# A linear-attention and GELU feed-forward kernel on one core: the first product of each pair slot reads its weights from another place in the ring

## The chip, the cores and the metric

The kernel runs on one core of a Trainium2 chip. The metric is device time in microseconds (us); lower is better. A profile is one execution recorded by the hardware; its times are us unless marked ns. TensorE does the matmuls (PE in the profile; its weight loads, which run beside matmuls, are PEld), VectorE is DVE, ScalarE is ACT, GpSimd is POOL, and SyncE is SP, whose queue issues the transfers here.

## What is computed

Per head, `kv = k^T v`, `out = q kv`, an RMS norm over the 64 head columns with a gain, and then a feed-forward layer with GELU over all 4608 tokens:

```python
kv = np.einsum('bhsd,bhse->bhde', k, v)          # batch 8, heads 8, seq 576, head_dim 64
out = np.einsum('bhsd,bhde->bhse', q, kv)
rms = np.sqrt(np.mean(out * out, axis=-1, keepdims=True) + 1e-06)
x = (out / rms * g_norm) as (4608, 512)
h = x @ w_in                                      # 512 x 2048
g = 0.5 * h * (1.0 + erf(h / sqrt(2)))
return g @ w_out                                  # 2048 x 512
```

## The kernel before

**Tiles and stages.** The 4608 tokens are nine chunks of 512 (CH). A weight block of `w_in` is 128 of the 2048 hidden columns, 16 blocks in all; `w_out` has 16 blocks likewise, which stay on the chip. For accuracy every operand is kept as two float32r parts, a high one and the rest (hi, lo), and a product takes three matmuls: hi by hi, lo by hi, hi by lo.

**The two plain chunks (c = 0, 1).** The first layer (line 537) multiplies whole blocks; the second layer (line 563) adds into four PSUM tiles `acc`. In chunk 1, TensorE and VectorE also form sums and differences of quarters of `w_in`, and SP stores them as 28 tiles `products` in device memory (lines 366 to 419).

**The pair chunks (c = 2 to 8).** From chunk 2 on, two blocks of the first layer are taken together as a pair, with seven products of half size in place of eight (Strassen's scheme in Winograd's form). There are 8 pair slots a chunk and 7 chunks, 56 slots. In a slot, `layer1_pair` (line 429) runs products 0 to 6 in order. Product k takes six matmuls of line 444: two halves of the contraction, three part products each. The stationary operand (`lhsT`, 128x128) is a quarter block of the weights from `products`; the moving operand (`rhs`, 128x256) is a piece of x. After the slot's seven products come the second layer's matmuls of earlier blocks (line 563, 128x512, mostly 24), in some slots a projection of the next chunk (line 218) or sums for kv (line 158). VectorE combines the products in PSUM meanwhile (lines 436 and 454), and ScalarE applies GELU (lines 549, 550).

**Which tiles are moving operands.** `piece_tile` (line 359) gives them: in even chunks product 0 reads x2, product 1 x3 and the others w_in5 to w_in9, in odd chunks product 0 to 3 read x0, x1, x4, x5 and the others w_in10 to w_in12. The names w_in4 and up are old weight tiles used again.

**The ring.** The weights of the products come back through a ring of RING = 4 tiles, w_in0 to w_in3. Each is 1024 + ROOM = 1088 elements of 4 bytes a partition. One transfer of 512 KB fills a tile with two products in a row, numbers n = 2t and 2t + 1 of the whole run, at the elements AWAY = 48 to 48 + 1024. So product n stands 192 bytes into its tile if n is even, and 192 + 2048 if it is odd. `load_products(t)` (line 423) is called for tile t + 4 when the second product of tile t has been written out as code, so the transfer waits on TensorE for that product's end. As a slot has seven products, product 0 of a slot is the first half of a tile in every second slot and the second half in the others.

**Addresses.** In the built program the four ring tiles and all the tiles with moving operands start at byte addresses that leave the same remainder, 192, on division by 256; so do the `w_out` tiles and the GELU results gh and gl, the operands of lines 563 and 584. Blocks inside tiles start at multiples of 512 bytes from there.

**What sets the order.** The schedule is written by hand. Each engine runs its instructions in program order and waits on semaphores. SP issues all transfers in program order: the ring loads, the kv and q loads of later chunks (lines 103 to 193) and the output stores (line 605). The transfers take the semaphores DMAHW0 to DMAHW7 in turn, so a transfer may have to wait until an earlier one with its semaphore has landed.

**The end.** `finish` (line 569) runs the last chunk's last blocks; its last output tile is done in two halves of 256 columns, 12 matmuls of 128x256 on line 584, with gh or gl as stationary and `w_out` as moving operand.

Of the kernel before, what the change touches and what calls it, by code (L numbers as in the profile page):

```python
# [8 lines left out]
F32 = mybir.dt.float32  # L9
# [15 lines left out]
RING = 4  # L25
# [11 lines left out]
def linear_attn_rms_gelu_ffn(  # L37
# [16 lines left out]
    nc = tc.nc  # L54
    ctx.enter_context(tc.manual_schedule())
    NT, DM = out.shape
# [26 lines left out]
    AWAY, ROOM = 48, 64  # L83
# [265 lines left out]
    NPR = len(OPERANDS)  # L349
    NT2 = NPR * NF // 4  # L350
    kept = {}

    def reused(i, dtype=F32):

        if i not in kept:
            kept[i] = block_tile(f"w_in{i}", dtype)
        return kept[i][:, :2 * DM]
# [6 lines left out]
    products = [dram.tile([P, 2 * DM], F32, name=f"products{t}") for t in range(NT2)]  # L364
# [56 lines left out]
    ring = {}  # L421

    def load_products(t):
        if t < (NCH - PLAIN) * NT2:
            reused(t % RING, F32R)
            ring[t] = kept[t % RING][:, AWAY:AWAY + 2 * DM]
            nc.sync.dma_start(out=ring[t].bitcast(F32), in_=products[t % NT2])

    def layer1_pair(at, j, between):


        a, b = (ps_h.tile([P, CH], F32, name="ps_h") for _ in range(2))
        left, right = slice(0, HALF), slice(HALF, CH)
        u = reused(15).rearrange("p (a n) -> p a n", n=HALF)
        p1, u2, v, u3 = (u[:, i] for i in range(4))
        add = lambda out, x, y: nc.vector.tensor_tensor(out=out, in0=x, in1=y, op=ALU.add)  # L436

        def product(k, out, first=False):
            n = ((at.c - PLAIN) * NF // 2 + j) * NPR + k
            w, x = ring[n // 2][:, n % 2 * DM:(n % 2 + 1) * DM], at.x[k]  # L440
            for kb in range(2):
                hi, lo = (w[:, m * HALF + kb * P:m * HALF + (kb + 1) * P] for m in range(2))
                for i, (y, z) in enumerate(((hi, 0), (lo, 0), (hi, 1))):
                    nc.tensor.matmul(  # L444
                        out=out, lhsT=y, rhs=x[:, z, kb], start=first and kb + i == 0,
                        stop=kb == 1 and i == 2, skip_group_check=True,
                    )
            if n % 2:
                load_products(n // 2 + RING)

        between[0]()
        product(0, a[:, left], True)
        product(1, a[:, right])
        nc.vector.tensor_copy(out=p1, in_=a[:, left])  # L454
        add(v, a[:, right], p1)
        product(2, b[:, right], True)
        product(3, b[:, left])
        add(u2, b[:, right], p1)
        between[1]()
        product(4, a[:, left])  # L460
        product(5, a[:, right])
        add(a[:, right], a[:, right], u2)
        product(6, b[:, right])
        add(u3, b[:, right], p1)
        add(b[:, left], b[:, left], u3)
        add(b[:, right], b[:, right], v)
        return a, b
# [141 lines left out]
    first, second = attn[:2]  # L609
# [49 lines left out]
    for d in range(0, 2 * D, BLK):  # L659
        h = d // D * D  # L660
        nc.gpsimd.tensor_tensor(
            out=fold[:, d:d + BLK], in0=ident[:, h:h + BLK], in1=ident[:, h + BLK:h + 2 * BLK],
# [25 lines left out]
    n = 2 * NB  # L688


    def sum_squares(p):
# [13 lines left out]
        out=half_g, in0=ps[:, :1], scalar1=0.5, scalar2=None, op0=ALU.mult  # L705
# [3 lines left out]
        out=sums[:, :P], lhsT=ones, rhs=eps, start=True, stop=False,  # L709
# [4 lines left out]
        out=root_g, in0=half_g, scalar1=D ** 0.5, scalar2=None, op0=ALU.mult  # L714
# [8 lines left out]
    for p in (2, 3):  # L723
# [5 lines left out]
        out=sums[:, :n].rearrange("p (g b) -> p g b", g=2), lhsT=fold, rhs=first.part[:, :2, :],  # L729
# [3 lines left out]
    for p in (2, 3):  # L733
        nc.scalar.activation(
            out=first.o_tile(p), in_=first.ps.pop(p), func=AF.Copy, scale=root_g
# [9 lines left out]
    for p in (2, 3):  # L745
        bcs[p] = ps_acc.tile([P, DM], F32, name=f"acc{p}")
        for t in range(NG):
            for h, r in enumerate((slice(0, D), slice(D, 2 * D))):
                k = n + 2 * ((p - 2) * NG + t) + h
                nc.tensor.matmul(  # L750
                    out=bcs[p][r, t * P:(t + 1) * P],
# [3 lines left out]
    for p in range(2):  # L755
# [3 lines left out]
            out=first.o_tile(p), in0=first.ps.pop(p), scalar=root_g, in1=bc, op0=ALU.mult,  # L759
# [86 lines left out]
    def later(c, i):  # L846

        if i == 9:
            sums[c] = attn[c + 1].fold()
        if i in (5, 7):  # L850
            load_kv(c + 2, (i - 5) // 2)
        if i == 9:
            attn[c + 2].load(0)
        if i == 13:
            for p in (2, 3):
                load_kv(c + 2, p)
        if i == 15:
            attn[c + 2].load(1)
        if i == 13:
            for t in range(RING):  # L860
                load_products(t)
# [36 lines left out]
    for s in range(PLAIN * NF):  # L898
# [36 lines left out]
        else:  # L935
# [3 lines left out]
            n = 0 if not 1 <= i <= 11 else 2 if i in (1, 3, 5, 7, 11) else 1  # L939
# [114 lines left out]
```

## Time and profile before

| What | Value |
| --- | --- |
| Median of 3 runs | 830.99 us (830.6 to 831.09) |
| The profiled execution | 830.12 us |
| Its span, first to last instruction | 828.3 us |
| Granted TensorE clock | 1.000 over the span |
| Ring loads (line 427) | 196 of 512 KB, median 4.6 us from issue to landing |
| Products written (line 370) | 40 and 16 of 256 KB |

How to read it. A row of a group gives line, engine, operation, what is written `<-` what is read (with buffer numbers left out), the shape and the count; then durations. Matmuls overlap their neighbours, since they are pipelined, so the duration of one says less than the distance from one start to the next. The chain of waits follows the work that ended last back through what released it; its rows in order of time are start, length and how many instructions. A row of a timeline is start, length and instructions merged. In a row of transfers, "landing" counts from the issue on the queue to the semaphore that tells of the last byte.

### The profile page before, as it was taken

The numbers are of one execution on the slowest core, as the hardware profiler recorded it, in microseconds if no ns is written. First come the engines' busy times: TensorE is split into PE (matmuls) and PEld (weight loads), VectorE is DVE, ScalarE is ACT, GpSimd is POOL, SyncE is SP. The second block draws the span as 40 slices with busy tenths as digits, with TensorE's granted clock in tenths as the row PEclk, the third lists the DMA queues.
The fourth block names the chain that finished last, engine by engine and source line by source line (L and its number), as shares of the span: only waits on it lengthen the run. The fifth ranks groups of instructions, "written<-read, shape, count | busy, mean of one in ns | idle before, by whom it ended". The sixth has DMA issues, their size and how long they took to land.

```text
span 828.3 us, 13810 instructions
## 1 busy us (share of the span) xinstructions
PE 823.5 (99%) x5390; PEld 730.1 (88%) x5390; DVE 496.3 (60%) x980; ACT 314.0 (38%) x578; POOL 65.7 (8%) x69
## 2 busy tenths in 40 slices
PE   9999999999999999999999999999999999999998
PEld 7688888888999999999999999999999989999997
DVE  3999838687546744675457544673467456744443
ACT  3788444434531334233423253233323332322221
POOL 1000021001010100010100110010101000100000
PEclk9999999999999999999999999999999999999999
DMA  9981337776684568555945688456445665556551
GB/s 352 406 334 51 115 127 248 253 262 241 228 318 129 184 237 306 177 178 204 327 163 176 204 276 279 140 176 238 171 173 177 227 202 178 178 178 229 178 178 51
DMA packets 61605, 174.97 MB, mean 211 GB/s; under 512 B 6500, under 2 KB 15460, under 8 KB 61540
## 3 DMA queue, kind: packets, MB, share of 16 engines
q1 hardware_dynamic: 61536, 174.09, 60.2%
q8 instruction: 43, 0.70, 0.3%
q14 instruction: 22, 0.18, 0.1%
q10 hardware_dynamic: 4, 0.00, 0.0%
HBM read 149.95 MB, written 24.12 MB: 210 GB/s over the span
## 4 chain that ended last, share of the span: by engine, by line
PE 99%; DVE 0%; issue 0%; ACT 0%; DVEq 0%
PE acc L563 48%; PE ps_h L444 33%; PE ps_h L537 10%; PE ps_a L218 3%; PE ps_a L158 2%; PE ps_h L529 1%; PE ps_h L648 1%; PE acc L682 0%; PE acc L750 0%; PE ps_h L694 0%; PE ps_a L248 0%; DVE w L602 0%; DVE sq L591 0%; DVE z L592 0%; ACT w L595 0%
## 5 line engine op out<-in xcount | busy, mean ns | idle before, releaser
L563 PE MATMUL acc<-w_out,gh 128*128 128x512 f32 x700 | 216.7, 391 | 0.0
L444 PE MATMUL ps_h<-w_in,w_in 128*128 128x256 f32 x1392 | 172.9, 279 | 0.0
L444 PEld LDWEIGHTS ps_h<-w_in,w_in 128*128 128x128 f32 x1392 | 167.8, 188 | 0.0
L563 PE MATMUL acc<-w_out,w_in 128*128 128x512 f32 x672 | 159.3, 391 | 0.0
L563 PEld LDWEIGHTS acc<-w_out,gh 128*128 128x128 f32 x700 | 129.2, 188 | 25.2
L563 PEld LDWEIGHTS acc<-w_out,w_in 128*128 128x128 f32 x672 | 123.9, 188 | 24.6
L563 PE MATMUL acc<-w_out,gl 128*128 128x512 f32 x350 | 136.4, 390 | 0.0
L549 ACT ACTIVATE gh<-ps_h 128x512 fp32r<-128x512 f32 x88 | 52.6, 597 | 209.2 <-DVE ps_h L436 153.4
L444 PEld LDWEIGHTS ps_h<-x,w_in 128*128 128x128 f32 x960 | 120.9, 188 | 4.3
L444 PE MATMUL ps_h<-x,w_in 128*128 128x256 f32 x960 | 122.2, 279 | 0.0
L454 DVE COPY w_in<-ps_h 128x256 f32<-128x256 f32 x56 | 23.8, 425 | 131.5 <-PE ps_h L444 131.5
L549 ACT ACTIVATE w_in<-ps_h 128x512 fp32r<-128x512 f32 x56 | 33.5, 598 | 182.0 <-DVE ps_h L436 182.0
L436 DVE TENSOR_TENSOR ps_h<-ps_h,w_in 128x256 f32<-128x256 f32 x168 | 72.7, 432 | 46.1 <-PE ps_h L444 42.2
L436 DVE TENSOR_TENSOR w_in<-ps_h,w_in 128x256 f32<-128x256 f32 x168 | 71.4, 425 | 46.8 <-PE ps_h L444 44.9
L537 PE MATMUL ps_h<-x,w_in 128*128 128x512 f32 x360 | 86.8, 390 | 0.0
L550 ACT ACTIVATE ps_h<-ps_h 128x512 f32<-128x512 f32 x144 | 85.5, 594 | 0.0
L555 DVE TENSOR_TENSOR gl<-ps_h,gh 128x512 fp32r<-128x512 f32 x88 | 60.4, 687 | 41.6 <-ACT ps_h L550 37.3
L537 PEld LDWEIGHTS ps_h<-x,w_in 128*128 128x128 f32 x360 | 67.4, 188 | 14.0 <-POOL x L306 0.2
L563 PEld LDWEIGHTS acc<-w_out,gl 128*128 128x128 f32 x350 | 65.7, 188 | 14.3 <-DVE gl L555 0.3
L555 DVE TENSOR_TENSOR w_in<-ps_h,w_in 128x512 fp32r<-128x512 f32 x56 | 38.4, 686 | 17.1 <-ACT ps_h L550 17.1
L206 POOL TENSOR_TENSOR ql<-q,qh 128x512 fp32r<-128x512 f32 x16 | 21.3, 1330 | 209.3 <-ACT qh L205 139.4
L341 POOL TENSOR_TENSOR w_in<-o,w_in 128x512 fp32r<-128x512 f32 x13 | 16.9, 1321 | 209.7 <-ACT w_in L336 209.7
(153 smaller groups left out, 641.3 us busy)
## 6 DMA issues: line engine op xcount, KB each, us to landing
w_in<-products SPq DMA_DIRECT2D x196, 512.0 KB, 4.6
products<-w_in SPq DMA_DIRECT2D x40, 256.0 KB, 3.3
w_in<-w_in SPq DMA_DIRECT2D x16, 512.0 KB, 10.2
kv_main<-kv_main SPq DMA_DIRECT2D x16, 512.0 KB, 6.9
w_out<-w_out SPq DMA_DIRECT2D x16, 512.0 KB, 10.2
q<-qT SPq DMA_DIRECT2D x15, 512.0 KB, 6.1
out<-w SPq DMA_DIRECT2D x18, 256.0 KB, 2.1
out<-z SPq DMA_DIRECT2D x17, 256.0 KB, 2.3
```

Of the source, the lines that this page charges most:

```text
L158: nc.tensor.matmul(out=ps[r, n * D:(n + 1) * D], lhsT=k[:, r], rhs=v[:, r], start=(j == 0), stop=(j == NJ),)
L206: eng.tensor_tensor(out=ql, in0=q, in1=qh.bitcast(F32), op=ALU.subtract)
L218: nc.tensor.matmul(out=ps[:, a:e], lhsT=w, rhs=x[:, a:e], start=(m == 0), stop=(m == 2))
L341: eng.tensor_tensor(out=x[:, 1], in0=self.block(OPERANDS[n]), in1=x[:, 0].bitcast(F32), op=ALU.subtract,)
L436: add = lambda out, x, y: nc.vector.tensor_tensor(out=out, in0=x, in1=y, op=ALU.add)
L444: nc.tensor.matmul(out=out, lhsT=y, rhs=x[:, z, kb], start=first and kb + i == 0, stop=kb == 1 and i == 2, skip_group_check=True,)
L454: nc.vector.tensor_copy(out=p1, in_=a[:, left])
L537: nc.tensor.matmul(out=h, lhsT=parts["in", i][:, w][:, p * P:(p + 1) * P], rhs=at.x[p][:, x], start=(m + p == 0), stop=(m == 2 and p == NP ...
L549: nc.scalar.activation(out=gh, in_=h, func=AF.Gelu)
L550: nc.scalar.activation(out=h, in_=h, func=AF.Gelu)
L555: nc.vector.tensor_tensor(out=gl, in0=h, in1=gh.bitcast(F32), op=ALU.subtract)
L563: nc.tensor.matmul(out=ps, lhsT=x[:, ts], rhs=parts["out", i][:, w], start=(i == 0 and m == 0), stop=(m == 2 and (i == NF - 1 or (i, t) == ...
```

## The change

`load_products` treats a tile that holds a slot's product 0 (n divisible by NPR = 7) in another way. Product 0 is put at the place that a tile without the shift of 48 elements would give it: at element 0 if it is the first half, and at 512 + ROOM = 576 if it is the second, byte 2304, which is nine times 256. Its neighbour in the tile stays where it was, 48 or 560 elements in. As the two halves are no longer one stretch, such a tile is loaded in two transfers of 256 KB. All other tiles are loaded as before. The ring now holds one view for each product, which `product` takes out by its number.

```diff
     def load_products(t):
         if t < (NCH - PLAIN) * NT2:
             reused(t % RING, F32R)
-            ring[t] = kept[t % RING][:, AWAY:AWAY + 2 * DM]
-            nc.sync.dma_start(out=ring[t].bitcast(F32), in_=products[t % NT2])
+            to, src = kept[t % RING], products[t % NT2]
+            first = [not n % NPR for n in (2 * t, 2 * t + 1)]
+            for a in range(2):
+                at = a * DM + (a * ROOM if first[a] else AWAY)
+                ring[2 * t + a] = to[:, at:at + DM]
+            if any(first):
+                for a in range(2):
+                    nc.sync.dma_start(
+                        out=ring[2 * t + a].bitcast(F32), in_=src[:, a * DM:(a + 1) * DM]
+                    )
+            else:
+                nc.sync.dma_start(out=to[:, AWAY:AWAY + 2 * DM].bitcast(F32), in_=src)
...
             n = ((at.c - PLAIN) * NF // 2 + j) * NPR + k
-            w, x = ring[n // 2][:, n % 2 * DM:(n % 2 + 1) * DM], at.x[k]
+            w, x = ring.pop(n), at.x[k]
```

In the changed file the lines behind this place stand ten further down, so line 444 becomes 454 and line 563 becomes 573.

TensorE's instructions keep their order. At the start of the second slot of chunk 2, where product 0 is the second half of a ring tile (w_in with a number; x_1971 is its moving operand), they were, with the semaphores each waits for in brackets:

```order
L563 MATMUL acc_1368<-w_out_1224,gl 128x512
L444 MATMUL ps_h<-x_1971,w_in_2051 128x256 [waits DVE_49,PE_49]
L444 MATMUL ps_h<-x_1971,w_in_2051 128x256 x5
L444 MATMUL ps_h<-x_2068,w_in_1483 128x256 [waits DMAHW1_49]
L444 MATMUL ps_h<-x_2068,w_in_1483 128x256 x5
L444 MATMUL ps_h<-w_in_2071,w_in_1483 128x256 [waits DVE_49]
```

and they are now:

```order
L573 MATMUL acc_1368<-w_out_1224,gh 128x512 x2
L573 MATMUL acc_1368<-w_out_1224,gl 128x512
L454 MATMUL ps_h<-x_1971,w_in_2052 128x256 [waits DMAHW1_49,DVE_49,PE_49]
L454 MATMUL ps_h<-x_1971,w_in_2052 128x256 x5
L454 MATMUL ps_h<-x_2070,w_in_1483 128x256 [waits DMAHW3_49]
L454 MATMUL ps_h<-x_2070,w_in_1483 128x256 x5
L454 MATMUL ps_h<-w_in_2073,w_in_1483 128x256 [waits DVE_49]
```

Product 0 has a wait of its own for the transfer of its half (DMAHW1); before, the product ahead of it in the same tile had waited for the whole.

On SP, at the first kv loads of chunk 2 (products with a number are the 28 tiles in device memory, 81 the first), there stood:

```order
L427 DMA w_in_2051<-products_88 128x1024 [waits DMAHW0_49,PE_49]
L427 DMA w_in_1483<-products_89 128x1024 [waits DMAHW1_49,PE_49]
L427 DMA w_in_1492<-products_90 128x1024 [waits DMAHW2_49,PE_49]
L427 DMA w_in_2049<-products_91 128x1024 [waits DMAHW3_49,PE_49]
L124 DMA kv_main<-kv_main 128x1024 [waits DMAHW4_49]
L141 DMA kv_tail<-kv_tail 128x256 [waits DMAHW5_49]
L124 DMA kv_main<-kv_main 128x1024 [waits DMAHW6_49]
L141 DMA kv_tail<-kv_tail 128x256 [waits DMAHW7_49]
L103 DMA z<-kv_main 128x512 [waits DMAHW0_49,DVE_49]
```

and now:

```order
L433 DMA w_in_2052<-products_88 128x512 [waits DMAHW2_49,PE_49]
L433 DMA w_in_2052<-products_88 128x512 [waits DMAHW3_49,PE_49]
L437 DMA w_in_1483<-products_89 128x1024 [waits DMAHW4_49,PE_49]
L437 DMA w_in_1492<-products_90 128x1024 [waits DMAHW5_49,PE_49]
L433 DMA w_in_2050<-products_91 128x512 [waits DMAHW6_49,PE_49]
L433 DMA w_in_2050<-products_91 128x512 [waits DMAHW7_49,PE_49]
L124 DMA kv_main<-kv_main 128x1024 [waits DMAHW0_49]
L141 DMA kv_tail<-kv_tail 128x256 [waits DMAHW1_49]
L124 DMA kv_main<-kv_main 128x1024 [waits DMAHW2_49]
L141 DMA kv_tail<-kv_tail 128x256 [waits DMAHW3_49]
L103 DMA z<-kv_main 128x512 [waits DMAHW4_49,DVE_49]
```

Two of the four ring loads are now two transfers each. The z load took semaphore DMAHW0 after the load of products_88; now it takes DMAHW4 after the load of products_89.

## The prediction

> **What bounds the kernel now.** First the page, for the engine that carries the span; then the chain of waits, for what ends last; then single lines and stretches of the timeline, for the distance between matmuls.
>
> ```profile
> span 828.3 us, 13810 instructions
> PE 823.5 (99%) x5390; PEld 730.1 (88%) x5390; DVE 496.3 (60%) x980; ACT 314.0 (38%) x578; POOL 65.7 (8%) x69
> PEclk9999999999999999999999999999999999999999
> PE 99%; DVE 0%; issue 0%; ACT 0%; DVEq 0%
> PE acc L563 48%; PE ps_h L444 33%; PE ps_h L537 10%; PE ps_a L218 3%; PE ps_a L158 2%; PE ps_h L529 1%; PE ps_h L648 1%; PE acc L682 0%; PE acc L750 0%; PE ps_h L694 0%; PE ps_a L248 0%; DVE w L602 0%; DVE sq L591 0%; DVE z L592 0%; ACT w L595 0%
> ```
>
> The chain that ended last is TensorE for 99% of the span, at the full granted clock throughout. A transfer or a vector operation counts here only if TensorE comes to wait for it; otherwise the time is the number of matmuls times the distance from one start to the next. The change touches the second largest share, line 444: 2352 matmuls, 42 in each of 56 slots.
>
> ```profile
> 798.74 4.94 PE ps_h L444 x42
> 803.68 5.45 PE acc L563 x24
> ...
> 814.08 9.54 PE acc L563 x42
> ```
>
> The chain in order of time alternates. A slot's 42 matmuls of line 444 take 4.94 us, so 4.94 / 42 = 117.6 ns from start to start; 24 of line 563 take 5.45 us, 227 ns each. That is even from a slot's first matmul on, as TensorE's timeline of the same slot says:
>
> ```profile
> 798.58 1.58 PE L444 MATMUL ps_h<-x,w_in 128*128 128x256 f32 x12
> 799.99 3.69 PE L444 MATMUL ps_h<-w_in,w_in 128*128 128x256 f32 x30
> 803.52 0.63 PE L563 MATMUL acc<-w_out,gh 128*128 128x512 f32 x2
> ```
>
> Twelve starts (products 0 and 1) in 799.99 - 798.58 = 1.41 us are 117.5 ns each, the other thirty in 3.53 us 117.7. No wait for data hides in the first product:
>
> ```profile
> L444 PE MATMUL ps_h<-x,w_in x960: 279/279/280, 208.8 to 810.3; 128*128 128x256 f32 x192
> L444 PEld LDWEIGHTS ps_h<-x,w_in x960: 187/188/188, 208.6 to 810.1; 128*128 128x128 f32 x192
> ```
>
> All 960 matmuls with an x tile as moving operand, product 0 of every second chunk among them, were recorded at 279 to 280 ns and their weight loads at 187 to 188 (minimum, median, maximum). There is no slow first product to repair.
>
> **The change, part by part: the new place.** Product 0 keeps its 6 matmuls a slot, 56 x 6 = 336 in all, with the same shapes and order. Only the byte address of the stationary operand moves. In the program as built, the ring's tiles and all tiles with moving operands of line 444 start at a remainder of 192 on division by 256. AWAY is 48 elements, 192 bytes, so today a stationary operand stands at remainder 128 and its moving operand at 192. After the change product 0 stands 0 or 2304 bytes into its tile, at remainder 192, like its moving operand. Does line 444 ever show that pairing? No. But one line runs matmuls of the same 128x256 shape with both operands at remainder 192: line 584, the last output tile.
>
> ```profile
> L584 PE MATMUL acc<-w_out,gh x4: 277/282/283, 823.4 to 823.9; 128*128 128x256 f32 x4
> L584 PEld LDWEIGHTS ps_h<-w_out,gh x4: 192/192/192, 824.0 to 824.5; 128*128 128x128 f32 x4
> ...
> 823.44 0.40 PE L584 MATMUL acc<-w_out,gh 128*128 128x256 f32 x2
> 823.68 0.28 PE L584 MATMUL acc<-w_out,gl 128*128 128x256 f32 x1
> ...
> 824.76 0.28 PE L584 MATMUL ps_h<-w_out,gl 128*128 128x256 f32 x1
> ```
>
> From the third start to the twelfth, nine distances take 824.76 - 823.68 = 1.08 us: **120.0 ns** each, with weight loads of 192 ns instead of 188 and matmuls of 283 instead of 279. So my nearest row says that equal remainders cost 120.0 - 117.6 = 2.4 ns a matmul. Line 584 differs in more than the address (other tiles, often the same stationary block twice), so this is a likeness and no proof.
>
> The sum for one slot: six distances at 120.0 are 720 ns against 6 x 117.6 = 706. Two corrections. The first matmul after 512-wide ones is shorter: line 584's minimum of 277 against 283 is 6 ns, and product 0 too follows 512-wide matmuls. And the weights loaded beside product 0's last matmul are product 1's, at the old remainder, so I give that distance 117.6, 2.4 less. That leaves 720 - 6 - 2.4 = 711.6, or 6 ns a slot and 56 x 6 = **+0.3 us**.
>
> Both ends of this unknown: all six at 120.0 is 56 x 14.4 ns = +0.8 us. If all six took the short distance, 114, that is 56 x 6 x -3.6 ns = -1.2 us. Above that I add a disturbance of product 1 by the step back. The nearest row is the step from line 444 into line 563: 24 matmuls in 5.45 us there against 24 x 9.54 / 42 = 5.45 in the long run, so no more than the last digit, 10 ns a slot, 0.6 us. The ends are -1.2 and +1.4; I take +0.3, from the nearest row.
>
> The Trainium skill speaks against any effect: "TensorE: Matmul & The Clock Gate", section "Step-by-step: what each phase is for", gives TensorE two independent read ports, one for the streaming operand and one for the weights, so where one stands should not matter to the other, and the sum would be 0. The trace has 117.6 and 120.0 ns for one shape, which that alone doesn't explain.
>
> **The change: two transfers.**
>
> ```profile
> w_in<-products SPq DMA_DIRECT2D x196, 512.0 KB, 4.6
> L427 SPq DMA_DIRECT2D w_in<-products x196: 319/320/666, 194.6 to 803.0; - x196
> L427 SPq EVENT_SEMAPHORE  x194: 17/17/28, 194.5 to 802.3; - x194
> SPq L427 <- PE ps_h L444: 428.6, 183, 9.3
> ```
>
> There are 56 first products, each in a tile of its own, so 56 of 196 loads become two: 56 more issues of 0.32 us and some 44 waits of 17 ns on SP, about 19 us on a queue that stands 428.6 us waiting for TensorE to free a ring tile (183 waits). The bytes are the same, and 256 KB halves replace 512 KB. So the second half should land about 0.32 + 0.02 us later than the whole did; it may be as much as one further landing, 4.6 us, if the two ran one after the other, and nothing if halves land faster. I take 0.35.
>
> The cover: a tile is loaded again when its second product ends, and used after three other tiles, that is six products (6 x 706 ns = 4.24 us) and usually the 24 matmuls of line 563 (5.45 us): 9.7 us against 4.6. The tightest place is the start of chunk 2, where only 12 of line 563 and one projection stand between slots:
>
> ```profile
> 208.97 4.95 PE ps_h L444 x42
> 213.91 0.77 PE ps_a L218 x6
> 214.68 2.75 PE acc L563 x12
> 217.43 4.95 PE ps_h L444 x42
> ```
>
> There the interval is 4.24 + 2.75 + 0.77 = 7.8 us, less the 0.4 us until SP has issued; a landing of 4.6 leaves 2.8, of which 0.35 goes. The other crowded place is behind the kv loads, where SP also waits for an older transfer before it uses that one's semaphore again:
>
> ```profile
> SPq L103 <- DMA w_in<-products: 5.0, 6, 1.4
> 230.86 3.15 SPq L427 DMA_DIRECT2D w_in<-products  x3
> DMA to landing us min/median/max: 6.2/6.4/6.5
> 240.61 4.95 PE ps_h L444 x42
> ```
>
> The first of these three loads is issued at 230.9, lands by 237.4 and is used by the second product of the slot at 240.6, so at 241.3: 3.9 us of cover. With one ring transfer more ahead, the z load waits for the load of products 89 instead of 88, one tile or 2 x 706 ns = 1.4 us younger, and two more issues stand ahead (0.7 us): 2.1 us later at worst, 1.8 us left. So the cost is 0. Were the cover gone, TensorE would wait for the excess, once a chunk, and everything behind it on the chain with it.
>
> TensorE has as many wait instructions as before. Where product 0 is a tile's second half, it now waits for its own transfer; before, the product ahead of it had waited for both. Nothing is queued behind that wait but the slot itself, and by the cover above it is over before it is reached.
>
> **Sum.** The profiled execution took 830.12 us (span 828.3 and 1.8 around it); 830.12 + 0.3 = 830.4. It lies 0.87 below the median of the three runs, 830.99, and a measured median will stand like that one: **831.3 us**.
>
> **The rivals.**
> *The address is nothing*, and line 584's 120.0 comes from its other tiles: 830.99 + 0 = 831.0. For it speaks that line 563 and line 444 both keep even distances on whatever tile they read; against it, the 4 ns of difference in the weight loads. Chance 0.20. This is also the result by the skill's two read ports.
> *The short first distance wins*: product 0 falls to 114 to 117 ns and gains 0.1 to 1.2 us, 829.8 to 830.9. Against it, only one matmul of line 584 is that short. Chance 0.09. If the whole slot kept 114: 56 x 42 x 3.6 ns = 8.5 us, 822.5. Chance 0.05.
> *Slower: the 120 ns rhythm stays.* If loads and matmuls, once in step with equal remainders, don't fall out of it when product 1 goes back to the other remainder, all 42 run at 120.0: 56 x 42 x 2.4 ns = 5.6 us, 836.6. It decides at the seventh matmul of a slot: 120 there means this case. Against it, line 444 falls into its own distance at once after line 563, whose operands have equal remainders too (1.41 us for the first twelve). Chance 0.05.
> *Slower: the halves land one after the other*, 4.6 + 4.6 + 0.4 = 9.6 us. The 9.7 of an ordinary slot still covers it; the 7.4 at the tight place doesn't, 2.2 us twice: 835.4. It decides at a landing of 7.4 us. SP's idle time and the equal number of bytes speak against it. Chance 0.03.
>
> **How the numbers follow.** The forecast has 0.58, 831.0 to 831.8. Range: the low end is 829.8 less 0.3 for the scatter of medians (three runs spread 0.5), 829.5; the high end 830.99 + 1.4 and the scatter, 832.6. That leaves out the two slower cases and the fast slot, 0.13, and some tails. A measurement here tells about 0.2% from no change, 1.7 us: faster by more is 0.05, slower by more 0.05 + 0.03 = 0.08, the rest 0.87.
>
> **What would show it.** In the changed profile, the first six matmuls of each slot at about 119 ns, the other 36 at 117.6; weight loads up to 192 ns in product 0 and nowhere else in the slot; chain pieces of 42 at 4.94 to 4.96 us; halves that land in 5 us or less, and no wait of TensorE at a product's start. A 42-piece of 5.04 us means the rhythm stays; one of 4.94 with weight loads all at 188, that the address is nothing; a gap before a product, that the halves are late. All of this is wrong if line 584's distance has another cause that line 444 shares in the opposite sense.

## The result and the profile after

| | before | changed |
| --- | --- | --- |
| Median | 831.04 us (830.6 to 831.53, 4 runs) | 822.83 us (822.74 to 823.47, 4 runs) |
| The profiled execution | 830.12 us | 823.47 us |
| Its span | 828.3 us | 821.7 us |

The changed kernel takes 0.9903 of the time before (95% interval 0.989 to 0.9915): 8.2 us less. The prediction had 0.3 us more and a range down to 829.5; it was wrong. One of the four executions of e4 below took 2117.45 us; its median is of all four, its ratio of the other three.

The page of the changed kernel (instructions, then busy time and share of the span by engine) still has TensorE busy from end to end, with the same 5390 matmuls in 7.5 us less than before:

```profile
span 821.7 us, 13904 instructions
PE 816.0 (99%) x5390; PEld 721.8 (88%) x5390; DVE 496.1 (60%) x980; ACT 313.8 (38%) x578; POOL 65.7 (8%) x69
```

Its chain in order of time (start, length, what) shows the place. A slot's 42 matmuls (line 444, now 454) fell from 4.94 us to 4.79, and the 24 behind them (line 563, now 573) grew by 0.01:

```profile
210.35 4.79 PE ps_h L454 x42
...
797.23 5.46 PE acc L573 x24
802.69 4.79 PE ps_h L454 x42
807.49 9.56 PE acc L573 x42
```

TensorE's timeline of one slot, as it was shown of before, tells which part of the slot got faster:

```profile
792.27 1.56 PE L454 MATMUL ps_h<-x,w_in 128*128 128x256 f32 x12
793.66 3.56 PE L454 MATMUL ps_h<-w_in,w_in 128*128 128x256 f32 x30
797.06 0.63 PE L573 MATMUL acc<-w_out,gh 128*128 128x512 f32 x2
```

The first twelve starts, products 0 and 1, take 793.66 - 792.27 = 1.39 us, where they took 1.41. The other thirty take 797.06 - 793.66 = 3.40 us, 113.3 ns each, where they took 3.53. **The gain lies in the matmuls whose operands the change didn't move.** The single instructions of the line (minimum, median and maximum in ns) say the same:

```profile
L454 PEld LDWEIGHTS ps_h<-w_in,w_in x1392: 187/188/188, 211.5 to 807.1; 128*128 128x128 f32 x199
L454 PE MATMUL ps_h<-w_in,w_in x1392: 276/276/278, 211.6 to 807.2; 128*128 128x256 f32 x199
L454 PEld LDWEIGHTS ps_h<-x,w_in x960: 187/188/192, 210.0 to 803.7; 128*128 128x128 f32 x192
L454 PE MATMUL ps_h<-x,w_in x960: 276/276/283, 210.2 to 803.8; 128*128 128x256 f32 x192
```

Before, these matmuls were recorded at 277 to 280 ns. Now there are two kinds. By the trace's single records, product 0's first matmul takes 277 or 278 ns and its other five 282 or 283; the weight loads of 192 ns are the fourth to the seventh of each slot, the last of which is product 1's first. All other matmuls take 276 to 278, with weight loads of 187 or 188.

Where the records' own starts are averaged over the 56 slots, matmul by matmul, the distances in ns are:

```
                     1st  2nd  3rd  4th  5th  6th    7th to 42nd    a slot
before              117.5 118.4 117.5, and so on repeating           4945
changed             113.5 119.1 120  120  120  120.9  113.3 each     4794

the first five of the 24 512-wide matmuls behind a slot (the 32 slots that have these directly behind)
before              232.5 230.8 226.7 226.6 226.7                    1143
changed             232.3 235.9 228.2 232.6 230.9                    1160
```

Each of the 56 slots gains 151.6 ns, and where 512-wide matmuls stand directly behind, the first five give 16.6 back: 56 x 0.1516 - 32 x 0.0166 = 8.0 us. From the start of the first slot to the last piece's start the two chains differ by just that, (814.08 - 208.97) - (807.49 - 210.35) = 8.0 us, and the medians by 8.2.

The first slot starts at 210.35 us instead of 208.97, so the two profiled executions differ by only 6.65 us. In the other profiled executions below it started between 209.1 and 211.2. In the changed kernel's, 0.8 us of the delay is one wait of TensorE shortly ahead of the first slot, for a kv load (from the list of its waits; the profile of before has no such wait):

```profile
PE ps_a L158 <- DMA w_in<-kv_tail: 0.8, 1, 0.8
```

The first ring loads, six transfers now instead of four, are issued right behind that kv load. But e1 below issues the same six and has no such wait, so it is not shown that they delay it.

The two transfers cost TensorE nothing inside the slots, though they landed later than forecast (one line's instructions on SP's queue, then its landings; line 433 issues halves, line 437 whole tiles; two views of the changed kernel):

```profile
L433 SPq DMA_DIRECT2D w_in<-products x112: 319/320/1144, 195.1 to 787.0; - x112
DMA to landing us min/median/max: 2.5/4.9/8.2
```

```profile
L437 SPq DMA_DIRECT2D w_in<-products x140: 319/320/598, 196.2 to 796.6; - x140
DMA to landing us min/median/max: 3.1/4.6/8.7
```

A half lands 4.9 us after its own issue. The second half is issued 0.7 us behind the first, and by the trace's single records it lands 6.3 us (median) after the first one's issue: 1.7 us later than the 4.6 of a whole tile before. No distance inside a slot is longer than 121 ns, so TensorE waits at no product's start.

### The profile page after: what moved, and what is told of

Same layout as the page of the kernel before. It is cut to its first block, busy times and chain, and to the rows that moved or that the text cites. A ratio compares the mean times of both kernels' runs of the same rounds, so it can differ in the third digit from the quotient of the medians.

```text
span 821.7 us, 13904 instructions
## 1 busy us (share of the span) xinstructions
PE 816.0 (99%) x5390; PEld 721.8 (88%) x5390; DVE 496.1 (60%) x980; ACT 313.8 (38%) x578; POOL 65.7 (8%) x69
## 4 chain that ended last, share of the span: by engine, by line
PE 94%; DMA 2%; DVE 2%; issue 1%; SPq 0%; ACT 0%; DVEq 0%; ACTq 0%
PE acc L573 46%; PE ps_h L454 33%; PE ps_h L547 8%; PE ps_a L218 3%; PE ps_a L158 2%; PE ps_h L539 1%; DMA w_in<-kv_tail 1%; DMA out<-z 1%; PE ps_h L658 1%; PE acc L692 0%; DMA q<-qT 0%; DVE w_in L414 0%; DVE w L398 0%; DMA products<-x 0%; DVE gl L565 0%
## 5 line engine op out<-in xcount | busy, mean ns | idle before, releaser
L454 PE MATMUL ps_h<-w_in,w_in 128*128 128x256 f32 x1392 | 166.9, 276 | 0.0
L454 PEld LDWEIGHTS ps_h<-w_in,w_in 128*128 128x128 f32 x1392 | 161.9, 188 | 0.0
L454 PEld LDWEIGHTS ps_h<-x,w_in 128*128 128x128 f32 x960 | 119.0, 189 | 4.4
L454 PE MATMUL ps_h<-x,w_in 128*128 128x256 f32 x960 | 119.8, 278 | 0.0
L547 PEld LDWEIGHTS ps_h<-x,w_in 128*128 128x128 f32 x360 | 67.4, 188 | 13.9 <-POOL x L306 0.2
```

The costliest lines, as they stand in the source:

```text
L454: nc.tensor.matmul(out=out, lhsT=y, rhs=x[:, z, kb], start=first and kb + i == 0, stop=kb == 1 and i == 2, skip_group_check=True,)
L547: nc.tensor.matmul(out=h, lhsT=parts["in", i][:, w][:, p * P:(p + 1) * P], rhs=at.x[p][:, x], start=(m + p == 0), stop=(m == 2 and p == NP ...
```

## The experiments

Ten different kernels were run beside the kernel before, one of them twice, and the changed kernel once more. "Equal" and "unequal" below say whether the addresses of the stationary and the moving operand leave the same remainder on division by 256. The moving operands of slots and second layer stood at remainder 192 in every kernel; of these matmuls only stationary operands were moved. For brevity "short step" is the distance of 113.3 ns, "long step" the 117.7 of before.

| kernel | edit | median, us | ratio to before, 95% | a slot, ns |
| --- | --- | --- | --- | --- |
| e1 | two transfers, old addresses | 830.63 | 0.9995 [0.9986, 1.0004] | 4945 |
| e2 | new addresses, one transfer | 823.06 | 0.9906 [0.9892, 0.9921] | 4793 |
| e3 | product 3 equal, not product 0 | 832.25 | 1.0014 [1.0005, 1.0024] | 4948 |
| e4 | all products equal | 836.25 | 1.0061 [1.0044, 1.0078] | 5033 |
| e5 | 2 half-width matmuls ahead of the slot | 832.72 | 1.002 [1.0011, 1.0029] | 4945 |
| e6 | 4 half-width matmuls ahead | 822.42 | 0.9895 [0.988, 0.991] | 4760 |
| e7 | 6 half-width matmuls ahead | 822.86 | 0.99 [0.9884, 0.9917] | 4760 |
| e8 | 3 of product 0's 6 equal | 822.29 | 0.9893 [0.9878, 0.9908] | 4773 |
| e9 | e8, gh and gl moved | 827.89 | 0.9958 [0.9942, 0.9975] | 4948 or 4773 |
| e12 | e8, the rest 64 bytes to the other side | 831.86 | 1.0007 [0.9997, 1.0017] | 4947 |

(The slots of e9 are of two kinds, 26 of 4948 ns and 30 of 4773 on average. For e5 to e7 the first slot, which has no halves ahead, is left out.)

### Transfers or addresses: e1 and e2

e1 keeps the two transfers and puts product 0 back to where it was:

```diff
-                at = a * DM + (a * ROOM if first[a] else AWAY)
+                at = a * DM + AWAY
```

> The 56 tiles with a product 0 are loaded in two transfers, but every product stands 192 bytes in, as before. Rhythm theory (product 0 at the old place only sets the step in which products 1 to 6 then run, 113.3 ns or 117.7 ns from start to start with the same addresses): 42 matmuls of a slot in 4.94 us, 831.0 us. Place theory (the blocks' distance in the tile itself makes the others faster): the same, 831.0. Transfer theory (smaller transfers disturb TensorE's reads less): 113.3 ns in products 1 to 6, 4.79 us a slot, about 823.

e2 keeps the new addresses and loads both halves by one transfer, whose destination has a step of its own from half to half:

```diff
+            lo = 0 if first[0] else AWAY
+            apart = DM + (AWAY if first[0] else ROOM - AWAY if first[1] else 0)
+            both = to[:, lo:lo + 2 * DM].bitcast(F32)
+            both = bass.AP(both.tensor, both.offset, [both.ap[0], [apart, 2], [1, DM]])
+            nc.sync.dma_start(out=both, in_=src.rearrange("p (a n) -> p a n", a=2))
```

> The places are those of the changed kernel, but a tile with a product 0 is loaded in one transfer whose two halves land apart. Rhythm theory and place theory: 4.79 us a slot, 822.8 us, with 56 fewer issues on SP that nobody waits for. Transfer theory: 4.94 us a slot, 831.0.

e1 took 830.63 us, no change, and e2 823.06, the whole gain. A slot of each, from the chains in order of time of e1 and of e2:

```profile
778.13 4.94 PE ps_h L454 x42
```

```profile
781.78 4.79 PE ps_h L452 x42
```

The second transfer costs nothing and brings nothing: the cause is in the addresses alone.

### The same pairing elsewhere, and everywhere: e3 and e4

e3 gives the equal remainder to product 3 in place of product 0, in the middle of the slot:

```diff
-            first = [not n % NPR for n in (2 * t, 2 * t + 1)]
+            first = [n % NPR == 3 for n in (2 * t, 2 * t + 1)]
```

> Product 3 stands at the old place in place of product 0 (its tile is loaded in two transfers). Rhythm theory: products 0 to 2 keep 117.7 ns, product 3 about 119.5, products 4 to 6 fall to 113.3: 18 x 117.7 + 6 x 119.5 + 18 x 113.3 = 4.87 us a slot, about 828. If only a product straight behind the 512-wide matmuls can set the step (its first distance of 113 ns): 117.7 in all but product 3, 4.95 us a slot, 831.5. Place theory: product 3's neighbours in the tiles fall, products 0 and 1 too, 4.8 us, 823.

e4 is the kernel before with all seven products at the start of the tile, all equal:

```diff
-            ring[t] = kept[t % RING][:, AWAY:AWAY + 2 * DM]
+            ring[t] = kept[t % RING][:, :2 * DM]
```

> All products stand at element 0 of their tiles, so all stationary operands have the same remainder of 256 bytes as their moving operands. Rhythm theory with line 584 as its row: 113, 119 and then 40 times 120 ns, 5.03 us a slot, 56 x 0.09 = 5.0 us slower than before, 836. If the 120 ns came from other things than the address: 4.79 to 4.94 us a slot, 823 to 831.

e3 took 832.25 us. Its slot, in the chain in order of time:

```profile
779.91 4.95 PE ps_h L454 x42
784.85 5.49 PE acc L573 x24
```

By the averaged starts, product 3 shows the mark of equal remainders (116.7 118.3 119.2 120.8 116.7 118.3 ns), a disturbance of three matmuls follows (117.6 115.8 121.6), and then it is 117.7 again. So six equal matmuls aren't enough by themselves to bring the short step.

e4 took 836.25 us. The instructions of its line 444, and one slot of its chain:

```profile
L444 PEld LDWEIGHTS ps_h<-w_in,w_in x1392: 192/192/192, 210.8 to 819.8; 128*128 128x128 f32 x199
L444 PE MATMUL ps_h<-w_in,w_in x1392: 283/283/283, 210.9 to 819.9; 128*128 128x256 f32 x199
```

```profile
773.15 5.03 PE ps_h L444 x42
778.18 5.47 PE acc L563 x24
```

From a slot's fourth matmul on all weight loads take 192 ns, and the distance is 120.0 from the third matmul on: 42 x 120 = 5.04 us. Equal remainders do cost 120.0 ns a matmul, as line 584 had said of before. (Whether it is the equality that counts, or the stationary operand's own remainder of 192, is not shown, as no run moves a slot's moving operand.) With the stationary operand at remainder 128 there are two steady distances, 117.7 and 113.3, and the change put the slots from the one into the other.

### Opening the short step without touching a slot: e5, e6 and e7

In the kernel before, the last 512-wide matmuls ahead of a slot are each cut in two of 256 columns. Both operands of these are at remainder 192, as before. The ring, its addresses and all products stay as they were. e5 cuts one matmul, e6 two, e7 three (their operands are the GELU results and `w_out`); the edit of e6:

```diff
...
-                    nc.tensor.matmul(
-                        out=ps, lhsT=x[:, ts], rhs=parts["out", i][:, w],
+                    left -= 1
+                    wide = HALF if left < halves else DM
+                    for at in range(0, DM, wide):
+                        nc.tensor.matmul(
+                            out=ps[:, at:at + wide], lhsT=x[:, ts],
+                            rhs=parts["out", i][:, w.start + at:w.start + at + wide],
...
-            second_layer(due[0])
+            second_layer(due[0], halves=0 if due[1:] else 2)
...
-                second_layer(n)
+                second_layer(n, halves=0 if n != due[-1] else 2)
```

> The ring stays as in the kernel before. The last 512-wide matmul ahead of a slot is cut into two of 256 columns, whose operands have equal remainders. Locked-step theory (the 113.3 ns of products 1 to 6 are reached only from the step of 120 ns and weight loads of 192 ns, which four or more equal-remainder 256-wide matmuls behind 512-wide ones settle into): two are too few, 42 matmuls at 117.7, and 113 + 119 - 227 = 5 ns a slot more, 831.4. Trigger theory (any equal-remainder 256-wide matmul straight behind a 512-wide one will do): 42 at 113.3, 56 x (0.184 - 0.005 - 0.017 in the 512-wide ones behind) less, 822. Place theory (where product 0's block stands beside the others): 831.4.

> As the one before, with the last two 512-wide matmuls cut into four halves. Locked-step theory: four may be just enough (weight loads of 192 ns begin beside the fourth), then 42 at 113.3 and 113 + 119 + 120 + 120 - 453 = 19 ns more, 822.7; else 831.9. Trigger theory: 822.7. Place theory: 832.

> As before it, with the last three 512-wide matmuls cut into six halves: the same run of six that product 0 is in the changed kernel, though the ring is that of before. Locked-step and trigger theory: 42 at 113.3, 33 ns more for the halves and 33 less in product 0 than in the changed kernel, 822.8 to 823.5. Place theory: 832.9.

From the chains in order of time of e5, e6 and e7:

```profile
780.35 4.94 PE ps_h L444 x42
785.29 5.50 PE acc L568 x25
```

```profile
781.25 4.76 PE ps_h L444 x42
786.01 5.49 PE acc L568 x26
```

```profile
781.52 4.76 PE ps_h L444 x42
786.28 5.50 PE acc L568 x27
```

With two halves ahead the slot takes 4.94 us; with four or six it takes 4.76, all 42 matmuls at 113.3 ns. One slot in e6 and one in e7 stay long, the first, which follows a plain chunk and so has no halves ahead. In e6's chain:

```profile
209.94 4.95 PE ps_h L444 x42
```

Between e5 and e6 the code of the slot, its operands and its addresses are the same. So the distance of a matmul is not given by its own shape and addresses alone: what ran **ahead** of it sets which of two steps it takes, and it keeps that step through 42 matmuls, each with its own weights. This is the main finding. The piece of 26 or 27 behind shows what the halves and the way back into 512-wide matmuls cost, 0.04 to 0.05 us a slot; e5 pays it too.

Ahead of the other 55 slots the four halves of e6 run at 113.3, 119.2, 120.0 and 120.8 ns, like product 0 in the changed kernel; in e5 the two run at 113.2 and 121.8. So two equal 256-wide matmuls, run here as the halves of one 512-wide one, don't do. They leave a mark all the same: e5's slots last as long as those of before, yet the five 512-wide matmuls behind take 1159 ns instead of 1143. So two slots of the same length need not leave the same thing behind.

### How few of product 0: e8, e10 and e11

e8 starts from the changed kernel and keeps equal remainders only for the first half of product 0's contraction, three matmuls in place of six. The other three stand at AWAY like the rest of the ring; such a tile takes three transfers:

```diff
...
+                a = first.index(True)
+                olds, news = (0, HALF + AWAY) if a == 0 else (DM + ROOM + HALF, DM + AWAY)
+                ring[2 * t + a] = [
+                    [to[:, at + m * P:at + (m + 1) * P] for at in (olds, news)] for m in range(2)
+                ]
...
```

> From the changed kernel: only the first three matmuls of product 0 (first half of the contraction) read their weights at the old remainder, the other three at the remainder of products 1 to 6; such a tile is loaded in three transfers. Locked-step theory: three distances 113, 119, 120 are too few, 117.7 behind them, 831. Trigger theory: 39 at 113.3, 22 ns a slot less than the changed kernel, 821.6. Place theory: something between, by half the block, 827.

It took 822.29 us, against the expectation that three are too few: 113.3, 119.2, 120.8 ns, and then 39 matmuls at 113.3. Three equal matmuls are enough, and with three fewer at 120 ns the slot is 20 ns shorter than in the changed kernel. To tell these two apart, e8 and the changed kernel were run again, on one chip:

> The kernel with three old places once more, beside the changed kernel on the same chip: a slot of 4.77 us against 4.79, 56 x 0.020 = 1.1 us less than the changed kernel by the locked-step theory; if the extra transfers take that back, the same time.

> The changed kernel once more, to stand beside the one with three old places: 822.8.

e10, the same kernel as e8, took 821.78 us (820.91 to 822.5; ratio 0.9888 [0.9873, 0.9903]); e11, the changed kernel, 823.46 us (823.03 to 823.8; 0.9908 [0.9893, 0.9923]). The runs don't overlap, so the version with three equal matmuls beats both kernels, by 1.7 us against the changed one. The slots account for 56 x 20 ns = 1.1 of it. In the two profiled executions, 2.0 us apart, the rest lies ahead of the slots: the first one starts at 209.28 us in e10 and at 210.31 in e11. That part is not shown to come from the edit. e10's chain in order of time:

```profile
780.04 4.78 PE ps_h L468 x42
784.81 5.46 PE acc L587 x24
```

### What must run directly ahead: e9

e9 is e8 with an unused tile ahead of gh and gl, so that these stand at remainder 128 and their 512-wide matmuls with `w_out` (192) have unequal remainders. The GELU results of every second group of blocks lie in old weight tiles (named w_in in the rows) and stay equal. So slots of both kinds alternate in one execution:

```diff
+        if p == 3:
+            work.tile([P, AWAY], F32, name="gap")
```

> From the kernel with three old places: the GELU results gh and gl (stationary operands of 1050 of the 1722 512-wide matmuls) are moved by 192 bytes, so that their remainder is 128 beside 192 of the moving w_out. If the short step is open to 512-wide matmuls too (226.7 less 6.7 ns), 1050 x 6.7 = 7.0 us less, 815.3. If their distance does not depend on the address: 822.3. If slots behind such 512-wide matmuls no longer fall into the short step: up to 28 slots x 42 x 4.4 ns = 5.2 us more, 827.5.

It took 827.89 us, about half the gain. TensorE's timeline of two slots, the first behind gh and gl (unequal), the second behind w_in (equal):

```profile
765.21 0.62 PE L587 MATMUL acc<-w_out,gh 128*128 128x512 f32 x2
765.66 0.39 PE L587 MATMUL acc<-w_out,gl 128*128 128x512 f32 x1
765.89 1.58 PE L468 MATMUL ps_h<-x,w_in 128*128 128x256 f32 x12
767.31 3.69 PE L468 MATMUL ps_h<-w_in,w_in 128*128 128x256 f32 x30
770.84 5.61 PE L587 MATMUL acc<-w_out,w_in 128*128 128x512 f32 x24
776.29 1.54 PE L468 MATMUL ps_h<-x,w_in 128*128 128x256 f32 x12
777.67 3.56 PE L468 MATMUL ps_h<-w_in,w_in 128*128 128x256 f32 x30
781.07 0.62 PE L587 MATMUL acc<-w_out,gh 128*128 128x512 f32 x2
```

The thirty matmuls take 770.84 - 767.31 = 3.53 us in the first slot and 781.07 - 777.67 = 3.40 in the second. Product 0 is the same code with the same remainders in both, and every operand of a slot stands where it stood in e8 (the gap moves a few other working tiles too). So three equal 256-wide matmuls open the short step behind 512-wide ones that are equal too, in 27 of 27 slots, and mostly not behind unequal ones. There 26 slots are long and three are short, at 4774, 4774 and 4775 ns, with the same remainders as the 26. What sets the three apart is the last distance ahead of the slot: 226 ns, like the 226 or 227 behind equal ones, where the 26 have 230 to 236. This suggests, from three slots only, that the pace at the slot's start decides, and the address of the 512-wide matmuls only by way of it. Moving gh and gl brings nothing to the 512-wide matmuls themselves: the distances of the unequal ones are 226, 229 or 232 ns, 230 on average, against 227.

### The other side: e12

e12 is e8 with the rest of the ring 64 bytes above the moving operand's remainder (0 after 192) in place of 64 below (128):

```diff
-    AWAY, ROOM = 48, 64
+    AWAY, ROOM = 16, 64
```

> The kernel with three old places, with the other products 64 bytes into their tiles in place of 192, so 64 bytes after the moving operand's remainder instead of 64 before it. If any unequal remainder has the short step: 4.77 us a slot, 822. If the side matters: another distance, 115 to 120 ns in 39 matmuls of a slot, 826 to 836.

```profile
779.83 4.95 PE ps_h L468 x42
784.77 5.47 PE acc L587 x24
```

It took 831.86 us, no change. In this chain in order of time the slot takes 4.95 us, and after the three equal matmuls the distances are 117.5 and 118.3 ns. So the short step hangs on where the other products stand too. Weight loads of 192 ns occur among these long-step matmuls as well, 728 of 2352, so that duration is no mark of equal remainders alone. Whether the short step doesn't exist on this side, or wants another opening, one run can't tell.

## Why the prediction was wrong

**What held.** TensorE sets the time, at the full granted clock, and the transfers are hidden: e1 gives 0.9995, and TensorE waits for no half. The forecast 0.35 us for the later landing of the second half was too small, it was 1.7, but the 2.8 us of cover hid that. The new term itself was right in mechanism and size: product 0 was to take 711.6 ns a slot against 706 and took 713.5, at the 120 ns of line 584 and with a short first distance. Of its two corrections the first came (113.5 ns; 114 was forecast), the second didn't: the sixth distance is 120.9 and not 117.6. By that term alone the kernel would have lost 0.4 us. Two slips changed nothing: product 0 of every chunk, not of every second one, is among the 960 matmuls that read an x tile, and the upper end of the range adds up to 832.7, not 832.6.

**The step that failed** is the one on product 1 and the rest of the slot. The prediction took the 117.6 ns of the other 36 matmuls as fixed by their shape and addresses, and allowed only "a disturbance of product 1 by the step back", bounded by the last digit of the step from line 444 into line 563: 10 ns a slot. The measured effect of the step back is (113.3 - 117.7) x 36 = -158 ns a slot, sixteen times that bound and of the other sign; 56 of them are -8.9 us. With product 0's +6.8 ns (713.5 against a measured 706.7) and the +16.6 ns behind 32 of the slots that is the -8.0 us above. The 512-wide matmuls' part of it was in no term either.

**The nearest row was no bound.** 444 into 563 is a change of shape, from 256 to 512 columns. What the change does is go from equal to unequal remainders between 256-wide matmuls, and no row of before shows that: line 584 never goes back. So the prediction had a transition without a row and took the price of another transition for it.

**The rivals.** "The rhythm stays" had asked whether product 0 leaves a state behind that the other 36 keep, which was the right question, but only in one direction: towards the slower 120 ns, 836.6 us. That price was right for e4, where all products are equal: 836.25. "If the whole slot kept 114" was priced at 822.5 us, within 0.4 us of the result, at a chance of 0.05. That the number fits is luck: product 0 runs at 119, and only the 36 behind it at 113.3. Splitting ahead of the slot (e6) does give 42 at 113.3. The argument that set the slow rhythm aside, that line 444 falls into its own distance at once behind line 563, doesn't hold in general, as e5 and e6 show: there is no one distance of line 444's own.

**The address is nothing** was the rival with 0.20. From the two independent read ports that the Trainium skill names ("TensorE: Matmul & The Clock Gate", section "Step-by-step: what each phase is for") the prediction drew the same sum of 0. The runs disagree with that conclusion. Moving only stationary operands gives 120.0 ns (e4), 117.7 (before) or 113.3 (changed) for one shape and one order of instructions, and 836.25, 831.04 and 822.83 us.

**The sign that was asked for** did show it: the changed profile was to have "the other 36 at 117.6", and has 113.3.

**How far the cause is settled.** Shown: the addresses and not the transfers; two steps for the same matmuls, kept through a slot; the short one is opened by three, four or six equal 256-wide matmuls directly behind equal 512-wide ones, and not by two halves of one matmul, nor by six in the middle of a slot that runs at the long step (e3), nor, in 26 slots of 29, by three behind unequal 512-wide ones (e9). This fits the reading that weight loads and matmuls can run locked against each other in more than one order, and that a short stretch of a third pace moves them from one to the other; but that reading is argued from the distances only. Open are the mechanism, why three are enough and two aren't, whether 256 is the true period (stationary operands stood at remainders 0, 128 and 192 only), whether the moving operand's address counts at all, since the slots' never moved, and why the other side (e12) stays long.

## What to carry to other kernels

Where TensorE is busy throughout, read the distance from start to start, matmul by matmul through a block, and don't take an even distance for the only one that these operands have: the same 256-wide float32r matmuls ran at 117.7 or 113.3 ns, by what ran ahead of them and by where the stationary operand stood modulo 256 bytes, the moving one being at 192. Before laying out tiles, try a few offsets of the stationary operand and a few narrow matmuls ahead of a long block, since an offset of 192 bytes was worth 1% here. In a forecast, a transition that no row shows has an effect on everything that runs behind it; a safer bound is every distance that any row of that shape shows, times all of those matmuls, and not the price of the nearest other transition.

## What the runs showed of the hardware

In these kernels a stream of 128x256 float32r matmuls, each with its own weight load, has a memory: it keeps a step of 113.3 or 117.7 ns through a slot of 42 matmuls (e6, e5), at a granted clock of 1.000. With stationary and moving operand both at remainder 192 the step is a third, 120.0 ns, with weight loads of 192 ns in place of 188 (e4). The first five 512-wide matmuls directly behind a slot take 1143 ns in the kernel before and in e1, and 1160 in the changed kernel. That is no price of the short step alone: long-step slots pay it as well in e3, e5 and e12 (1159 to 1161). A load of 512 KB cut in two of 256 KB, 56 times, changed nothing that could be measured (e1: 0.9995).
